# Reading the next expert's gates and indices three places later in a delta-rule and mixture-of-experts kernel

## The chip, the cores and the metric

The kernel runs on one core of a Trainium2 chip. The metric is the device time of one execution in microseconds (us). The engines are named as in the profile: PE (TensorE) multiplies matrices, with PEld for its weight loads, DVE (VectorE) and ACT (ScalarE) work on elements, POOL (GpSimd) here issues the scattered writes of the output, and SP (SyncE) issues the other DMAs, one after the other in the order of the program.

## The reference, cut to what matters

```python
def _attn_ref(q, k, v, beta):                    # B, H, S, D = 4, 8, 768, 48
    k_n = k / (norm(k) + 1e-06)
    for t in range(S):                           # a state of 48 x 48 per batch and head
        y[:, :, t] = q_t @ state
        state = state + beta_t * outer(k_t, v_t - k_t @ state)

def _moe_ref(x, w_gate, w1, w2):                 # x: 3072 tokens x 384, 8 experts
    expert_idx = argmax(x @ w_gate); gate_w = softmax(x @ w_gate)[chosen]
    for e in range(8):
        xe = x[expert_idx == e]
        out[mask] = gate_w * (maximum(xe @ w1[e], 0) @ w2[e])   # 384 -> 1024 -> 384
```

The outputs are 3072 rows of 384 floats. All arrays are float32.

## The kernel before, in words

The first 290 us or so compute the attention part, a block of 128 positions at a time, choose an expert for each token and scatter each token's row (384 features, 8 gate logits, 2 words of index) into DRAM, into a list per expert of 448 slots. Most rows lie in `xg`; those of the last blocks lie in `xt`. A part of expert 0 runs beside it. The change does not touch this stage.

The second stage runs the experts 0 to 7 one after the other. `ffn` of an expert is cut into places: the loop of line 1134 gives it twelve, `t` = 0 to 11. At places 0 to 7 PE makes one 128-row block of the hidden layer each (line 785, nine matmuls of 448 columns: float32 is done as three products of a high and a low part), ACT takes the ReLU of it as the high part (line 788) and DVE makes the low part (line 789). Five PSUM banks hold hidden blocks that wait for ACT and DVE. At places 8 to 10 PE makes the three output blocks (line 1092, 24 matmuls each; their last three take block 7 of the hidden layer), DVE transposes and scales them (lines 1094 and 1095), and POOL scatters them to the output. Experts 1 to 6 have 144 such matmuls each.

Two streams of preparation for the next expert are woven in by hand, and their order on each engine is that of the program:

- The weights. Each step of `pieces` takes one raw piece (512 KB of `w1` or 384 KB of `w2`, tile `w1r` or `w2r`), casts it on ACT (line 656, high part), subtracts on DVE (line 657, low part), and issues the load of the piece three ahead (line 672), which goes into the buffer just read. An expert has seven pieces, three of `w1` and then four of `w2`. The tuples `PC0`, `PC1`, `PC2` and `PC` say at which places a step comes, for experts 0, 1, 2 and the later ones. At places 0 to 7 it stands behind the place's ReLU, so a cast that waits for its piece holds up the next ReLU on ACT.
- The tokens. `tokens(e + 1)` steps at the places in `TOK`. In `load_blocks` the first step issues four reads of the main rows (`xr<-xg`, 168 KB each, line 711), at place 1. The second, at place 2, issues four reads of the last rows (`xs<-xt`, 24 KB each, line 730) and then the reads of gates and indices: eight (lines 732 to 734), alternately 17.5 KB from `xg` into `xr` and 2.5 KB from `xt` into `xs`, in runs of ten floats. For expert 7 they are three (lines 736 to 738). At place 8 DVE adds the last rows in (line 1041) and transposes, ACT and DVE split into high and low parts; at place 9 the gates and indices are used (lines 1066 and 771 to 776).

All of these DMAs go through SP. A weight load waits there for the subtraction that frees its buffer, and what stands behind it in the program waits with it.

Pieces are numbered through all experts from 0; expert 2's are 14 to 20 and expert 3's 21 to 27. Below, load 15 is the load of piece 15. At expert 1 the steps at places 0, 1, 2, 4, 6, 7, 8, 9, 10, 10 handle pieces 10 to 19 and issue loads 13 to 22. At expert 2 the steps at places 0, 1, 3, 4, 6, 8, 9, 10 handle pieces 20 to 27 and issue loads 23 to 30.

Of the kernel before, what the change touches and what calls it, by code (L numbers as in the profile page):

```python
# [40 lines left out]
def deltanet_moe(ctx, tc, q, k, v, beta, w_gate, w1, w2, out):  # L41
# [78 lines left out]
    DEF = 2  # L120
    FP = 10
    AH = 3
    TOK = (1, 2, 8, 8, 8, 8, 8, 8, 8, 9)
    PC = (1, 3, 4, 6, 8, 9, 10)
    EU = 18
    TS = 8
    TOK0 = (0, 8, 8, 8, 8, 9, 9, 9, 10)
    PC0 = (0, 1, 3)
    PC1 = (0, 1, 2, 4, 6, 7, 8, 9, 10, 10)
    PC2 = (0, 1, 3, 4, 6, 8, 9, 10)  # L130
# [500 lines left out]
    def run(gen, steps=1):  # L631

        for _ in range(steps):
            if next(gen, tiles) is tiles:
                return False
        return True
# [60 lines left out]
    def read(out, in_):  # L697
        ins = nc.sync.dma_start(out=out, in_=in_)
        for x in put:
            tc.add_manual_dep(ins.ins, x.name, mybir.DependencyInfo(mybir.DependencyClass.Sync, mybir.DependencyReason.DATA),  # L700
                              reason="rows of every scatter")
# [5 lines left out]
    def turned(dram, e, t0, t1, x):  # L707

        rows = dram[e * CAP + 32 * t0:e * CAP + 32 * t1, :]
        for a in range(4):  # L710
            read(x[32 * a:32 * a + 32], rows[:, 96 * a:96 * a + 96].rearrange("(n t) c -> t n c", t=32))

    def gates(dram, e, sm):
        tail = dram[e * CAP + NG * 128:e * CAP + NG * 128 + 64, DM:ROW]
        read(sm, tail.unsqueeze(0).broadcast_to([2, 64, ROW - DM]))

    def load_blocks(e):
        X = xq_[e % 2].tile([128, (NG + 1) * ROW if e % 2 == 0 else NX + NT_ * (E + 2)], F32, name=f"xr{e}", tag="xr")
        x = X[:, 0:NX].rearrange("p (n c) -> p n c", n=NT_)
        m = NT_ if e < E - 1 else NG + 1  # L720
        sm = X[:, NX:NX + m * (E + 2)].rearrange("p (g c) -> p g c", g=m)
        XR[e] = (x, sm)
        turned(xg, e, 0, NT_, x)
        yield
        n = NT_ - 4 * NG
        xs = xp_.tile([128, (96 + ROW - DM) * n], F32, name=f"xs{e}", tag="xs")
        y, ym = xs[:, 0:96 * n].rearrange("p (n c) -> p n c", n=n), xs[:, 96 * n:96 * n + ROW - DM]
        if e < E - 1:
            ym = xs[:, 96 * n:(96 + ROW - DM) * n].rearrange("p (n c) -> p n c", n=n)
        turned(xt, e, 4 * NG, NT_, y)  # L730
        if e < E - 1:
            for a in range(4):
                for z, dram, t0 in ((sm, xg, 0), (ym, xt, 4 * NG)):
                    read(z[32 * a:32 * a + 32], dram[e * CAP + 32 * t0:e * CAP + CAP, DM:ROW].rearrange("(n t) c -> t n c", t=32))
        else:
            gates(xg, e, sm[:, NG])
            gates(xt, e, ym)
            read(sm[:, 0:NG], xg[e * CAP:e * CAP + NG * 128, DM:ROW].rearrange("(g p) c -> p g c", p=128))
        yield
        add_last(e, (y, ym))  # L740
        XM[e] = sm[:, 4 * NG:] if e < E - 1 else sm[:, NG], ym
# [296 lines left out]
    def add_last(e, xs):  # L1038
        todo = ((XR[0][:, NG], xs),) if e == 0 else ((XR[e][0][:, 4 * NG:], xs[0]),)
        for x, y in todo:  # L1040
            nc.vector.tensor_tensor(out=x, in0=x, in1=y, op=ALU.add)

    def tokens(e, X):
        if e == 0:
            xs = load_last(e)
            X.extend(X0["x"])
            yield
            add_last(e, xs)
            X.append(smalls(e, G0, NG + 1, xp_))
            return  # L1050
        yield from load_blocks(e)
        xh = xp_.tile([128, KD, CAP], F32R, name=f"xh{e}", tag="xh", bufs=2)
        xl = xp_.tile([128, KD, CAP], F32R, name=f"xl{e}", tag="xl", bufs=2)
        X[0:0] = [xh, xl]
        yield
        x, xd = XR[e][0], []
        for i in range(2 * KD):
            d = (0, 1, 0, 2, 1, 2)[i]
            if i in (0, 1, 3):
                xd.append(xp_.tile([128, CAP], F32, name=f"xd{e}_{d}", tag="xd", bufs=2))  # L1060
                nc.vector.transpose(out=xd[d].rearrange("p (n t) -> p n t", n=NT_),
                                    in_=x.rearrange("p n (t k) -> p k n t", k=KD)[:, d])
            else:
                split(xh[:, d], xl[:, d], xd[d])
            yield
        nc.vector.tensor_tensor(out=XM[e][0], in0=XM[e][0], in1=XM[e][1], op=ALU.add)
        X.append(smalls(e, 0, NT_ if e < E - 1 else NG + 1, xp_))
# [63 lines left out]
    for e in range(E):  # L1131
        tok = tok1 if e == 0 else tokens(e + 1, XX[e + 1]) if e + 1 < E else iter(())
        main = ffn(e, WW[e], XX[e])
        for t in range(KF + NG + 1):
            if e == 0 and t == TS:
                run(tok0)
            run(tok, (TOK if e > 0 else TOK0).count(t))
            w = (PC0, PC1, PC2, PC)[min(e, 3)].count(t)
# [166 lines left out]
```

## Time and profile before

| | |
|---|---|
| median of 3 runs | 540.11 us (539.44 to 541.98) |
| the profiled execution, its own time | 533.12 us |
| its span, first to last instruction | 531.4 us |
| mean granted clock of PE | 0.981 |
| PE, DVE, ACT, POOL busy | 94%, 74%, 50%, 34% |
| DMA queue of SP: packets, MB | 168468, 67.06 |

The profile is of one execution. Its own time is 1.7 us over its span and 7.0 us under the median of the other runs. Busy shares are means over stages that differ; the expert stage is read below by itself.

### The profile page before, as it was taken

The numbers are of one execution on the slowest core, as the hardware profiler recorded it, in microseconds if no ns is written. First come the engines' busy times: TensorE is split into PE (matmuls) and PEld (weight loads), VectorE is DVE, ScalarE is ACT, GpSimd is POOL, SyncE is SP. The second block draws the span as 40 slices with busy tenths as digits, with TensorE's granted clock in tenths as the row PEclk, the third lists the DMA queues.
The fourth block names the chain that finished last, engine by engine and source line by source line (L and its number), as shares of the span: only waits on it lengthen the run. The fifth ranks groups of instructions, "written<-read, shape, count | busy, mean of one in ns | idle before, by whom it ended". The sixth has DMA issues, their size and how long they took to land.

```text
span 531.4 us, 17329 instructions
## 1 busy us (share of the span) xinstructions
PE 501.0 (94%) x7164; PEld 447.0 (84%) x7172; DVE 390.8 (74%) x1110; ACT 266.9 (50%) x496; POOL 181.7 (34%) x244
## 2 busy tenths in 40 slices
PE   7789899999999999788999999997999999999995
PEld 4657798899999887787899999985999999999995
DVE  5999969879999999446553484787777786878420
ACT  4636566667666554467532463554353536444120
POOL 8011221143233142323211110047271727365462
PEclk9999999999999999899999899997999999999998
DMA  6969789789576855645412557386765847483010
GB/s 133 151 149 227 171 210 217 151 199 175 127 184 134 183 131 119 209 101 201 143 65 90 107 145 157 115 209 162 178 170 143 180 115 165 142 189 114 19 44 29
DMA packets 173253, 77.76 MB, mean 146 GB/s; under 512 B 150786, under 2 KB 166864, under 8 KB 173172
## 3 DMA queue, kind: packets, MB, share of 16 engines
q1 hardware_dynamic: 168468, 67.06, 54.5%
q0 software_dynamic: 4704, 9.57, 5.3%
q8 instruction: 57, 0.93, 0.7%
q14 instruction: 24, 0.20, 0.1%
HBM read 53.02 MB, written 24.37 MB: 146 GB/s over the span
## 4 chain that ended last, share of the span: by engine, by line
PE 67%; DVE 20%; issue 4%; DMA 4%; ACT 3%; POOL 1%; SPq 0%; DVEq 0%; POOLq 0%; ACTq 0%
PE h L785 18%; PE y L1092 16%; PE y L795 4%; DVE lw L391 4%; PE yp L511 4%; PE pq L277 3%; PE yp L492 3%; PE ks L476 3%; PE xp L537 3%; PE ks L451 3%; PE pg L277 2%; DVE ta L380 2%; PE ks L462 2%; PE ku L501 2%; DVE tc L401 2%
## 5 line engine op out<-in xcount | busy, mean ns | idle before, releaser
L798 POOL DMA_INDIRECT out_dram<-yo,idx x90 | 97.9, 1087 | 134.9 <-DVE yo L1095 85.7
L1092 PE MATMUL y<-hx,w2h 128*128 128x448 f32 x288 | 85.7, 375 | 3.1 <-ACT hx L788 2.2
L302 POOL TENSOR_SCALAR_AFFINE_SELECT pm<-pm 128x512 f32<-128x512 f32 x48 | 31.2, 649 | 147.5 <-DVE lw L391 24.4
L788 ACT ACTIVATE hx<-h 128x448 fp32r<-128x448 f32 (+1 forms) x64 | 32.6, 519 | 61.7 <-PE h L785 58.3
L1092 PEld LDWEIGHTS y<-hx,w2h 128*128 128x128 f32 x288 | 55.3, 193 | 9.4 <-ACT hx L788 3.0
L785 PE MATMUL h<-xh,w1h 128*128 128x448 f32 x168 | 61.6, 366 | 1.0 <-DVE hx L789 1.0
L785 PE MATMUL h<-xl,w1h 128*128 128x448 f32 x168 | 61.5, 366 | 0.0
L785 PE MATMUL h<-xh,w1l 128*128 128x448 f32 x168 | 61.5, 366 | 0.0
L789 DVE SCALAR_TENSOR_TENSOR hx<-h,hx 128x448 fp32r<-128x448 f32 (+1 forms) x64 | 37.0, 587 | 32.1 <-ACT hx L788 32.1
L480 ACT COPY u<-ks 32x384 f32<-32x384 f32 x96 | 45.1, 470 | 23.5 <-PE ks L476 19.8
L1092 PE MATMUL y<-hx,w2l 128*128 128x448 f32 x144 | 53.5, 371 | 0.0
L657 DVE TENSOR_TENSOR w2l<-w2r,w2h 128x768 fp32r<-128x768 f32 x32 | 36.4, 1141 | 12.4 <-ACT w2h L656 12.0
L657 DVE TENSOR_TENSOR w1l<-w1r,w1h 128x1024 fp32r<-128x1024 f32 x24 | 29.4, 1226 | 14.1 <-ACT w1h L656 13.9
L656 ACT CAST w2h<-w2r 128x768 fp32r<-128x768 f32 x32 | 35.5, 1130 | 4.3 <-DMA w2r<-in_moe_w_dram 4.3
L785 PEld LDWEIGHTS h<-xh,w1h 128*128 128x128 f32 x168 | 31.5, 188 | 4.1 <-DVE hx L789 1.4
L391 DVE TENSOR_TENSOR lw<-lw,ta 128x31 f32<-128x31 f32 (+7 forms) x96 | 33.9, 353 | 0.3
L785 PEld LDWEIGHTS h<-xh,w1l 128*128 128x128 f32 x168 | 31.5, 188 | 2.8
L785 PEld LDWEIGHTS h<-xl,w1h 128*128 128x128 f32 x168 | 31.5, 188 | 2.7
L257 ACT COPY gg<-pg 128x512 f32<-128x512 f32 x48 | 25.8, 588 | 15.6 <-PE pg L277 15.4
L380 DVE TENSOR_TENSOR ta<-lg,lw 128x31 f32<-128x31 f32 (+7 forms) x96 | 33.4, 348 | 0.2
L277 PE MATMUL pq<-qt,kt 64*128 64x128 f32 x384 | 30.5, 292 | 2.1 <-ACT gg L257 1.2
L294 ACT COPY pm<-pq 128x512 f32<-128x512 f32 x48 | 25.8, 589 | 12.3 <-PE pq L277 12.3
(184 smaller groups left out, 1092.6 us busy)
## 6 DMA issues: line engine op xcount, KB each, us to landing
w1r<-in_moe_w_dram SPq DMA_DIRECT2D x24, 512.0 KB
w2r<-in_moe_w_dram SPq DMA_DIRECT2D x32, 384.0 KB
xg<-zrow SPq DMA_DIRECT2D x7, 788.0 KB
xr<-xg SPq DMA_DIRECT2D x28, 168.0 KB
kn<-in_k_dram SPq DMA_DIRECT2D x24, 192.0 KB
qn<-in_q_dram SPq DMA_DIRECT2D x24, 192.0 KB
xn<-row SPq DMA_DIRECT2D x10, 394.0 KB
ku<-in_k_dram SPq DMA_DIRECT2D x20, 192.0 KB
```

The costliest lines, as they stand in the source:

```text
L277: nc.tensor.matmul(pg[a][:, p], lhsT=kt[r, p], rhs=xt[r, p], start=True, stop=True, tile_position=(64 * a, 0), skip_group_check=True)
L302: ins = nc.gpsimd.affine_select(out=pm[:, hs], in_=pm[:, hs], compare_op=ALU.is_gt, fill=0.0, base=0, pattern=[[0, NP], [1, C]], channel_m ...
L380: nc.vector.tensor_tensor(out=x, in0=lg[:, rows, c:c + 1].broadcast_to([128, m, w]), in1=lw[:, c:c + 1, cols].broadcast_to([128, m, w]), o ...
L391: nc.vector.tensor_tensor(out=y, in0=y, in1=x, op=ALU.subtract)
L480: nc.scalar.copy(out=uview(n)[r], in_=ks[r])
L656: nc.scalar.copy(out=hi, in_=src)
L657: nc.vector.tensor_tensor(out=lo, in0=src, in1=hi.bitcast(F32), op=ALU.subtract)
L785: nc.tensor.matmul(ps, lhsT=w[:, d, fs], rhs=x_[:, d], start=(n == 0), stop=(n == len(terms) - 1))
L788: nc.scalar.activation(out=hh, in_=ps, func=AF.Relu)
L789: nc.vector.scalar_tensor_tensor(out=hl, in0=ps, scalar=0.0, in1=hh.bitcast(F32), op0=ALU.max, op1=ALU.subtract)
L798: ins = nc.gpsimd.indirect_dma_start(out=out.rearrange("n (a c) -> (n a) c", a=k), out_offset=bass.IndirectOffsetOnAxis(ap=idx, axis=0), i ...
L1092: nc.tensor.matmul(ps, lhsT=w[:, f, 128 * d:128 * d + 128], rhs=h[:, f], start=(n == 0), stop=(n == len(terms) - 1))
```

## The change

The generator `load_blocks` gets one more `yield`, between the reads of the last rows and the reads of gates and indices, and `TOK` one more place, 5. So the main rows are still read at place 1 and the last rows at place 2, and the gates and indices at place 5. `TOK0`, which does the same for expert 1 while expert 0 runs, gets a second 0, so that there both parts are issued at place 0 as before, in the same order.

```diff
-    TOK = (1, 2, 8, 8, 8, 8, 8, 8, 8, 9)
+    TOK = (1, 2, 5, 8, 8, 8, 8, 8, 8, 8, 9)
...
-    TOK0 = (0, 8, 8, 8, 8, 9, 9, 9, 10)
+    TOK0 = (0, 0, 8, 8, 8, 8, 9, 9, 9, 10)
...
         turned(xt, e, 4 * NG, NT_, y)
+        yield
         if e < E - 1:
             for a in range(4):
                 for z, dram, t0 in ((sm, xg, 0), (ym, xt, 4 * NG)):
```

## Rows read from the trace of the kernel before

**Rows 1.** The page's slices, 13.3 us each: PE's busy tenths, its granted clock.

```profile
PE   7789899999999999788999999997999999999995
...
PEclk9999999999999999899999899997999999999998
```

**Rows 2.** Windows from one expert's first matmul to the next's (experts 1, 2, 3).

```profile
core 0: us, PE busy (x) PEld busy (x) DVE busy (x) ACT busy (x) POOL busy (x), PEclk, DMA share, GB/s
311.39:340.48 29.09, 29.09 (x145) 26.86 (x145) 18.89 (x29) 14.41 (x20) 0.92 (x1) 1.00 0.59 151
340.48:378.44 37.96, 33.84 (x146) 28.95 (x145) 30.33 (x47) 18.29 (x24) 17.00 (x14) 0.91 0.62 161
378.44:407.68 29.24, 29.24 (x145) 27.02 (x145) 22.93 (x34) 13.70 (x19) 14.67 (x14) 1.00 0.63 164
```

**Rows 3.** Timeline of PE at expert 2: start, duration, in brackets the idle time before.

```profile
350.91 0.47 PE L785 MATMUL h<-xh,w1h 128*128 128x448 f32 x1 [0.98 <-DVE hx L789]
...
364.50 0.74 PE L1092 MATMUL y<-hx,w2h 128*128 128x448 f32 x1 [2.20 <-ACT hx L788]
...
365.82 1.12 PE L1092 MATMUL y<-hx,w2h 128*128 128x448 f32 x2 [0.21 <-DVE hx L789]
```

**Rows 4.** The chain that ended last, the one DMA on it at expert 2.

```profile
354.59 8.18 DMA w2r<-in_moe_w_dram
```

**Rows 5.** Timeline of ACT: casts of pieces 14, 15 and 24, ReLUs of block 7.

```profile
326.11 1.05 ACT L656 CAST w1h<-w1r 128x1024 fp32r<-128x1024 f32 x1 [1.29 <-DMA w1r<-in_moe_w_dram]
327.07 0.54 ACT L788 ACTIVATE hx<-h 128x448 fp32r<-128x448 f32 x1
332.47 1.05 ACT L656 CAST w1h<-w1r 128x1024 fp32r<-128x1024 f32 x1 [4.87 <-DMA w1r<-in_moe_w_dram]
...
362.80 1.21 ACT L656 CAST w2h<-w2r 128x768 fp32r<-128x768 f32 x1 [2.55 <-DMA w2r<-in_moe_w_dram]
363.92 0.53 ACT L788 ACTIVATE hx<-h 128x448 fp32r<-128x448 f32 x1
```

**Rows 6.** Timeline of SP's issues at expert 1, from place 2 on.

```profile
319.39 3.17 SPq L698 DMA_DIRECT2D xs<-xt  x4
322.60 0.42 SPq L698 DMA_DIRECT2D xr<-xg  x1
...
326.11 0.30 SPq L698 DMA_DIRECT2D xs<-xt  x1
...
327.92 0.48 SPq L698 DMA_DIRECT2D xs<-xt  x1
328.49 0.85 SPq L672 DMA_DIRECT2D w1r<-in_moe_w_dram  x2
```

**Rows 7.** Windows before and at load 15's landing, and at expert 2; columns as in 2.

```profile
326.11:328.49 2.38, 2.38 (x13) 2.21 (x12) 1.29 (x2) 1.50 (x2) 0.00 (x0) 1.00 0.19 11
328.49:332.47 3.98, 3.98 (x22) 3.69 (x21) 0.47 (x1) 0.00 (x0) 0.00 (x0) 1.00 0.74 222
...
351.99:362.80 10.81, 9.58 (x44) 7.74 (x43) 6.74 (x9) 4.74 (x8) 8.94 (x7) 1.00 0.92 198
```

**Rows 8.** Timeline of SP's issues at expert 2: load 24, the fourth gate read.

```profile
354.59 0.93 SPq L672 DMA_DIRECT2D w2r<-in_moe_w_dram  x1
...
362.79 0.30 SPq L698 DMA_DIRECT2D xs<-xt  x1
```

**Rows 9.** Timeline of DVE: expert 1's rows added; gates of experts 3 and 5 used.

```profile
307.37 0.36 DVE L1041 TENSOR_TENSOR xr<-xr,xs 128x192 f32<-128x192 f32 x1
...
373.33 0.17 DVE L1066 TENSOR_TENSOR xr<-xr,xs 128x20 f32<-128x20 f32 x1
...
431.26 0.17 DVE L1066 TENSOR_TENSOR xr<-xr,xs 128x20 f32<-128x20 f32 x1
```

**Rows 10.** Timelines of SP: last gate read for expert 1, and for expert 5.

```profile
307.52 0.47 SPq L698 DMA_DIRECT2D xs<-xt  x1
...
420.01 0.48 SPq L698 DMA_DIRECT2D xs<-xt  x1
```

## The prediction

> **What bounds the kernel now.** I began with the page's slices. In the expert stage, slices 24 to 39, PE is at 9 tenths in every slice but one: slice 28, from 359 to 372 us, stands at 7 and its granted clock at 7 [rows 1]. (Slice 40 is the tail behind the last expert.) So a change in this stage is worth only what it does to that slice, or what new hole it makes elsewhere. Windows from one expert's first matmul to the next's give the size: experts 1 and 3 take 29.09 and 29.24 us with PE busy throughout, expert 2 takes 37.96, at a mean clock of 0.91 [rows 2]. Expert 2 loses 37.96 - 29.17 = 8.8 us.
>
> PE's timeline says what it waits for there: 0.98 us for DVE, which has not yet freed the first of five hidden blocks, at 350.91; 2.20 us for ACT's ReLU at 364.50; DVE's low part of the same block at 365.82 [rows 3]. The chain that ended last goes at this place through one DMA, a weight load from 354.59 to its landing [rows 4]. ACT shows the same from its side: the cast of piece 24 waited 2.55 us for that load, began at 362.80, and the ReLU of block 7 had to stand behind it until 363.92 [rows 5]. So preparation of expert 3 arrives late and holds up expert 2's own ReLU.
>
> Why is it late? I followed ACT back. At expert 1 it waited 4.87 us for load 15, until 332.47 [rows 5]. From there the steps stand in one row: each load waits for the subtraction three pieces before, each subtraction for its cast. And load 15 left SP only at 328.49, behind the eight reads of gates, which SP took from 322.60 to 328.40 to issue [rows 6]. In the last 2.4 us of this the DMA engines moved 11 GB/s, with loads 15 to 17 in the air they moved 222 [rows 7]. The bandwidth was there; the loads were not issued.
>
> SP's pauses between these reads follow a pattern: the fourth read goes out at 326.11, when load 14 lands and its cast begins [rows 5, 6], and at expert 2 the fourth goes out at 362.79, when load 24 lands [rows 5, 8]. Both times it is the eighth DMA behind that load. I read this as: a DMA of SP is not issued before the one eight places ahead has landed.
>
> **The change, part by part.** Nothing is removed or added in work. At each of experts 1 to 5, eight reads move from place 2 to place 5, at expert 6 three: 43 DMAs. In SP's order each group moves behind two weight loads (places 2 and 4 at expert 1, places 3 and 4 later). POOL's queue is not touched. At expert 0 both steps fall on place 0, in the old order: zero.
>
> *Expert 1.* Load 15 takes the first gate read's turn: 322.60 instead of 328.49 [rows 6]. From issue to landing it took 332.47 - 328.49 = 4.0 us [rows 5, 6], which from 322.60 gives 326.6. But load 14 lands ahead of it at 326.11, and 512 KB behind that at 222 GB/s [rows 7] take at most 2.3 us: 328.4. The cast of piece 15 stands behind block 7's ReLU, which ends at 327.07 + 0.54 = 327.6 [rows 5]. So the cast begins between 327.6 and 328.4 and not at 332.47: the preparation runs 4.1 to 4.9 us earlier. I take 4.4, nearer the late end, because load 16 shares the engines.
>
> The gate reads are then issued behind load 16. By the pattern of eight, the seventh waits for load 15 and the eighth for load 16, so load 17 leaves at about 330.5 instead of 329.4. With the same 4.0 us it lands at 334.5. Its cast comes only at place 9, which PE itself begins at 311.39 + 96 x 0.203 = 330.9 [rows 2], and on ACT and DVE behind all of place 8: the transposes and splits of expert 2's tokens and piece 16. That work hides it; without it, what it is late would be taken off the 4.4 us.
>
> *Expert 2.* With the whole row of steps 4.4 us earlier, PE's wait at 350.91 (0.98) is gone. What is late next is load 24. It stands behind the four main reads and load 23 in both orders, so it only moves with its row: from 362.80 to 358.4. How late is that for PE? At 29.17/144 = 0.203 us per matmul, the last of the first output block (72 + 23 matmuls behind 340.48 [rows 2]) is due at 340.48 + 95 x 0.203 = 359.8. It ran at 365.82 [rows 3], 6.0 late. So 6.0 of the 8.8 us are waiting and the other 2.8 are the clock; that a mean of 0.91 over 37.96 us is 3.4 us of missing clock [rows 2] bounds this. Afterwards the wait is 6.0 - 4.4 = 1.6 us, in two pieces for high and low part, each below the 0.98 that left the clock at 1.00 in the window that followed [rows 3, 7]. So I count no fall of the clock, and the gain is 8.8 - 1.6 = 7.2 us.
>
> Two unknowns stand around load 24. Three gate reads were in the air behind it and no longer are, which can only help: at most the 1.6 us that remain. Against it, load 25, and later load 26, now come right behind it. Do later DMAs take a share from earlier ones? While load 15's 512 KB landed, the queue moved 3.98 x 222 = 884 KB [rows 7], so 372 KB of the loads behind went with it: yes. The bounds are nothing and both loads' 768 KB at the 198 GB/s of this stretch [rows 7], 3.9 us. I take nothing, as load 25 leaves only after the last rows' reads, when load 24 is mostly through.
>
> The Trainium skill (DMA: Bandwidth & Descriptors, "Queues, rings and completion order") says that each DMA engine takes descriptors in the order of the ring, while a later one may finish its write first. By that alone the loads behind would cost load 24 nothing and the sum would stay 7.2; the 372 KB show that landings do mix, so the bound stays.
>
> *Experts 3 to 6.* The later loads leave about 4 us sooner, the reads later. PE is full there, so no gain. The cover is the time between the reads and their use: expert 5's last gate read is issued at 420.01 and its gates are used at 431.26, 11.3 us later [rows 9, 10]. Two hidden blocks, the distance from place 3 to place 5, are 2 x 9 x 0.203 = 3.7 us; so some 7.6 us remain: no cost. The adding of last rows at place 8 does not wait for the gates, though they share its tiles: for expert 1 it ran at 307.37, before the last gate read was even issued at 307.52 [rows 9, 10].
>
> **Sum.** 533.12 - 7.2 = 525.9 us for the profiled execution. The other runs' median is 7.0 us above it, for which the trace gives no reason; I take the same microseconds off: 540.1 - 7.2 = 532.9. The likeliest case's own range, with shifts of 3.5 to 5.5, is 532 to 534.5.
>
> **The rivals.**
> *The hole closes wholly.* Load 24 lands 1.6 us sooner than I say, for instance because no gate reads are in the air with it. For it: the reserve of DMA bandwidth at expert 1. Against: the main reads still lie before it. 540.1 - 8.8 = 531.3. Chance 0.25.
> *The hole shrinks, but the clock falls all the same.* If loads 25 and 26 cost load 24 about 0.6 us, PE's wait is 2.2, as long as the one after which the clock halved [rows 3]. Then 2.8 + 0.6 come back: 7.2 - 3.4 = 3.8, 536.3 us. Chance 0.14.
> *No difference.* Loads 25 and 26 take their full share: 1.6 + 3.9 = 5.5 us of waiting and 2.8 of clock against 8.8 leave 0.5 us; the stretch before load 24's landing ran at 0.92 of the DMA engines [rows 7], which speaks for it. Against: load 25 is issued behind load 24. 539.6 us. Chance 0.13.
> *Slower.* The gates come late. Their use at place 9 blocks DVE, and with it output blocks and the next ReLUs. This decides from about 7.6 us of landing time after the last issue; PE feels it only when its five free hidden banks, 5 x 1.83 us, are used up, less some 3 us until DVE's first low part, so from 13 or 14 us. Each further microsecond costs five at experts 2 to 6; 2 us beyond would give 540.1 - 7.2 + 10 = 543. Against: expert 3's gates, the latest now with their fourth read out at 362.79, were used at 373.33 with no wait [rows 8, 9]. Chance 0.06.
> The Trainium skill (DMA: Bandwidth & Descriptors, "Rules for kernel authors") would issue a DMA early and wait for it late, which speaks for this rival; here the trace shows early reads holding back loads that are more urgent.
>
> **How the numbers follow.** 0.42 is left for my forecast. A measurement of this kernel tells about 0.5% (2.7 us) from no change. Faster by more: 0.25 + 0.42 + 0.14 = 0.81; within it 0.13; slower 0.06. The range runs from the wholly closed hole with the runs' own lower spread (531.3 - 0.7 = 530.6) to the fallen clock with most of their upper spread (536.3 + 1.5 = 537.8); what is left out is about 2 in 10.
>
> **What would show it.** Right: ACT's wait of 4.87 us before piece 15 shrinks below 1 us; load 15 leaves SP before 324; between the last rows' and the gates' issues stand two weight loads; expert 2's block takes 30 to 31.5 us; clock 1.00 in slice 28. Wrong: cast 15 moves but load 24 still lands near 362 (DMA bandwidth, not order, was the limit); or a new wait at lines 1066 or 771 for a DMA; or expert 1, whole until now, gets a hole because load 14 shares with loads 15 and 16 and lands over 2.7 us later (block 7's ReLU, over at 327.6, is due at 311.39 + 93 x 0.203 = 330.3).

## The result, and the profile after

| | before | changed |
|---|---|---|
| median of 4 runs each, us | 539.78 (535.40 to 541.98) | 531.50 (528.53 to 533.22) |
| ratio, 95% interval | | 0.987 (0.9825 to 0.9915) |
| the profiled execution, its own time | 533.12 | 531.65 |

A ratio compares the fast executions of the two kernels only, leaving out the slow ones, which lie over 1.5% above the fastest, so 0.987 is not the quotient of the two medians. By the ratio the change is worth 539.8 x 0.013 = 7.0 us (4.6 to 9.4 by its interval); 7.2 were forecast, and the median of 531.5 stands 1.4 us under the 532.9. The two profiled executions, though, differ by only 1.5 us. Both facts have to come out of the trace.

The page's slices of the changed kernel, PE and its granted clock, to be held against [rows 1]:

```profile
PE   7799899999999999898999899999999999999975
...
PEclk9899999999999999999999999999999999999979
```

Slice 28 is full now, at full clock, and stays so to slice 38. A new dent stands in slice 39, near the end. Windows by expert, as in [rows 2], give the size of both: experts 1, 2 and 3, and from expert 7's first matmul to the end of the span.

```profile
core 0: us, PE busy (x) PEld busy (x) DVE busy (x) ACT busy (x) POOL busy (x), PEclk, DMA share, GB/s
311.19:340.43 29.24, 29.24 (x145) 27.02 (x145) 22.43 (x38) 17.03 (x24) 0.92 (x1) 1.00 0.64 164
340.43:370.03 29.60, 29.60 (x146) 26.96 (x145) 24.94 (x36) 15.84 (x21) 15.01 (x14) 1.00 0.69 185
370.03:399.28 29.25, 29.25 (x146) 27.03 (x145) 22.95 (x35) 13.65 (x19) 15.58 (x14) 1.00 0.66 162
...
487.17:529.90 42.73, 33.30 (x161) 30.65 (x159) 8.46 (x16) 6.68 (x12) 18.38 (x24) 0.91 0.09 28
```

Expert 2's block fell from 37.96 [rows 2] to 29.60: 8.4 us, and PE is busy for all of the 29.60. The last stretch took 42.73 us; in the profile of before the same stretch takes 35.82:

```profile
495.58:531.40 35.82, 29.95 (x160) 28.46 (x159) 8.46 (x16) 6.69 (x12) 18.52 (x24) 0.95 0.10 34
```

So 6.9 us went again, and 8.4 - 6.9 = 1.5 is what the pair of profiles shows. What the 6.9 are, runs 1 and 9 below tell: they come with the execution, not with the change.

ACT's timeline, to be held against [rows 5]: the casts of pieces 14, 15 and 24, the ReLU behind the last, and two ReLUs of expert 7.

```profile
326.16 1.05 ACT L656 CAST w1h<-w1r 128x1024 fp32r<-128x1024 f32 x1 [1.55 <-DMA w1r<-in_moe_w_dram]
327.12 0.54 ACT L789 ACTIVATE hx<-h 128x448 fp32r<-128x448 f32 x1
327.85 1.06 ACT L656 CAST w1h<-w1r 128x1024 fp32r<-128x1024 f32 x1 [0.19 <-DMA w1r<-in_moe_w_dram]
...
356.14 1.23 ACT L656 CAST w2h<-w2r 128x768 fp32r<-128x768 f32 x1 [2.11 <-DMA w2r<-in_moe_w_dram]
357.27 0.55 ACT L789 ACTIVATE hx<-h 128x448 fp32r<-128x448 f32 x1
...
505.36 0.54 ACT L789 ACTIVATE hx<-h 128x448 fp32r<-128x448 f32 x1 [4.38 <-remote]
508.95 0.54 ACT L789 ACTIVATE hx<-h 128x448 fp32r<-128x448 f32 x1 [3.04 <-remote]
```

The wait before piece 15 went from 4.87 to 0.19 us. Piece 24's cast still waits, 2.11 us, but 15.7 us after the block's start and no longer 22.3, in time for PE: no wait of PE is left in the blocks of experts 2 to 6. SP's issues at expert 1, as in [rows 6], and last one of expert 2:

```profile
322.64 1.57 SPq L672 DMA_DIRECT2D w1r<-in_moe_w_dram  x2
324.81 0.33 SPq L698 DMA_DIRECT2D xr<-xg  x1
326.16 0.33 SPq L698 DMA_DIRECT2D xs<-xt  x1
...
328.51 0.42 SPq L698 DMA_DIRECT2D xr<-xg  x1
329.44 0.30 SPq L698 DMA_DIRECT2D xs<-xt  x1
...
356.14 0.33 SPq L698 DMA_DIRECT2D xs<-xt  x1
```

Loads 15 and 16 stand ahead of the gate reads. The pattern of eight shows again: the second read goes out at 326.16 with the cast of piece 14, and at expert 2 the second at 356.14 with that of piece 24; before, it was the fourth each time [rows 6, 8], because loads 15 and 16, or 25 and 26, now stand between.

### The profile page after: what moved, and what is told of

Same layout as the page of the kernel before. It is cut to its first block, busy times and chain, and to the rows that moved or that the text cites. A ratio compares the mean times of both kernels' runs of the same rounds, so it can differ in the third digit from the quotient of the medians.

```text
span 529.9 us, 17343 instructions
## 1 busy us (share of the span) xinstructions
PE 500.8 (95%) x7172; PEld 446.0 (84%) x7172; DVE 388.2 (73%) x1110; ACT 267.0 (50%) x496; POOL 181.2 (34%) x244
## 4 chain that ended last, share of the span: by engine, by line
PE 71%; DVE 15%; ACT 4%; DMA 3%; issue 3%; POOL 2%; another core or an unknown queue 1%; SPq 0%; POOLq 0%; ACTq 0%; DVEq 0%
PE h L786 21%; PE y L1093 17%; PE y L796 4%; PE pg L277 4%; PE yp L492 3%; PE yp L511 3%; PE ks L476 3%; PE pq L277 3%; PE xp L537 3%; PE ks L451 3%; PE ks L462 2%; DVE lw L391 2%; DMA kn<-in_k_dram 2%; PE pt L230 2%; PE wm L650 1%
## 5 line engine op out<-in xcount | busy, mean ns | idle before, releaser
L1093 PE MATMUL y<-hx,w2h 128*128 128x448 f32 x288 | 82.8, 365 | 0.0
L1093 PEld LDWEIGHTS y<-hx,w2h 128*128 128x128 f32 x288 | 54.0, 188 | 4.4
L786 PEld LDWEIGHTS h<-xh,w1h 128*128 128x128 f32 x168 | 31.5, 188 | 2.8
L786 PEld LDWEIGHTS h<-xh,w1l 128*128 128x128 f32 x168 | 31.5, 188 | 2.8
L786 PEld LDWEIGHTS h<-xl,w1h 128*128 128x128 f32 x168 | 31.5, 188 | 2.8
L277 PE MATMUL pg<-kt 64*128 64x128 f32 x384 | 29.6, 292 | 2.6 <-ACT gg L257 2.2
L277 PE MATMUL pq<-qt,kt 64*128 64x128 f32 x384 | 29.6, 285 | 2.0 <-ACT gg L257 1.2
```

Source lines behind the costliest of these rows:

```text
L277: nc.tensor.matmul(pg[a][:, p], lhsT=kt[r, p], rhs=xt[r, p], start=True, stop=True, tile_position=(64 * a, 0), skip_group_check=True)
L786: nc.tensor.matmul(ps, lhsT=w[:, d, fs], rhs=x_[:, d], start=(n == 0), stop=(n == len(terms) - 1))
L1093: nc.tensor.matmul(ps, lhsT=w[:, f, 128 * d:128 * d + 128], rhs=h[:, f], start=(n == 0), stop=(n == len(terms) - 1))
```

## The experiments

The times of one kernel spread by up to 4% on the chips used here, so a ratio's interval is wide and the block of expert 2 in the profile is the sharper measure. The table gives it for all runs but run 10, with the time in it that PE was idle (the window's length less PE's busy time), and the cast of piece 15 after expert 1's first matmul and of piece 24 after expert 2's first matmul (ACT's timeline, minus the block's start), which is where loads 15 and 24 landed if ACT waited for them. A block's bounds are read to within one matmul, 0.2 us. Each row gives one profiled execution, and the ratio of the timed runs; runs 1 to 4, 5 to 8, and 9 and 10 stood on one chip each. Edits are shown against the changed kernel.

| run | gate reads | piece 15, us | piece 24, us | expert 2's block, us | PE idle in it, us | ratio to before (95%) |
|---|---|---|---|---|---|---|
| first profile of before | place 2 | 21.1 | 22.3 | 37.96 | 4.1 | 1 |
| 1, before again | place 2 | 21.0 | 21.8 | 36.12 | 4.1 | 1.0025 (0.9961 to 1.0089) |
| 3 | 2 at expert 1, then 5 | 21.2 | 21.1 | 35.98 | 4.2 | 0.9979 (0.9925 to 1.0032) |
| 4 | 2, in sixteen halves | 26.8 | 26.3 | 41.55 | 5.8 | 1.0135 (1.0091 to 1.0180) |
| changed | 5 | 16.7 | 15.7 | 29.60 | 0 | 0.9870 (0.9825 to 0.9915) |
| 5, changed again | 5 | 16.4 | 16.4 | 29.72 | 0 | 0.9940 (0.9880 to 0.9999) |
| 9, changed again | 5 | 16.7 | 16.8 | 30.10 | 0.2 | none |
| 2 | 5 at expert 1, then 2 | 16.4 | 17.3 | 30.66 | 0.6 | 0.9896 (0.9792 to 0.9999) |
| 6 | 3 | 16.7 | 17.7 | 31.08 | 0.9 | 0.9900 (0.9853 to 0.9947) |
| 7 | 8 | 16.5 | 16.8 | 30.10 | 0.6 | 0.9943 (0.9903 to 0.9983) |
| 8 | 5, in sixteen halves | 16.6 | 15.8 | 29.60 | 0 | 0.9956 (0.9914 to 0.9997) |

**Run 1: the kernel before again.** No edit.

> The kernel before, unchanged, to see a second profile of it and what two runs of one kernel differ by. Both theories: ratio 1.00 within 0.4%. Expert 2's block again takes 37 to 39 us, with load 24 landing about 22 us after the block's start (362.8 - 340.5 in the first profile) and piece 15's cast waiting about 4.9 us at expert 1. Open: whether ACT's pauses of 4.4 and 3.0 us at expert 7, which the profile of the changed kernel has and that of before has not, come with the execution and not with the change; then they may appear here too, and would explain the 7 us between the profiled execution of before and its other runs.

The windows of expert 2 and of the last stretch, and ACT at expert 7:

```profile
338.60:374.72 36.12, 32.05 (x146) 27.53 (x145) 28.91 (x46) 18.28 (x24) 15.33 (x14) 0.95 0.59 163
493.83:535.60 41.77, 32.16 (x161) 29.51 (x159) 8.46 (x16) 6.68 (x12) 18.38 (x24) 0.93 0.09 29
```

```profile
514.31 0.54 ACT L788 ACTIVATE hx<-h 128x448 fp32r<-128x448 f32 x1 [6.55 <-remote]
515.79 0.54 ACT L788 ACTIVATE hx<-h 128x448 fp32r<-128x448 f32 x1 [0.94 <-remote]
```

Two things follow. The hole at expert 2 varies between executions of one kernel: 36.1 here, under the 37 to 39 that were expected, and 38.0 in the first profile. PE was idle for the same time in both, 36.12 - 32.05 = 4.07 us here and 4.12 [rows 2]; what differs is how long it was busy, at a mean granted clock of 0.95 against 0.91. So the blocks of before and of the changed kernel lie 6.0 to 8.4 us apart, by the pair that one takes. And ACT's pauses at expert 7 stand in the kernel before too: the last stretch takes 41.77 us instead of 35.82. The first profile of before, at 533.12, lacked them. The 7.0 us between it and its other runs, for which the prediction found no reason, are about this size; that they are the cause is likely and not shown, as the other runs left no trace.

**Run 2: only expert 1's reads moved.**

```diff
-            run(tok, (TOK if e > 0 else TOK0).count(t))
+            run(tok, (TOK0 if e == 0 else TOK if e == 1 else (1, 2, 2, 8, 8, 8, 8, 8, 8, 8, 9)).count(t))
```

> Only the reads for expert 2 (issued at expert 1) stand at place 5; all later ones stay at place 2. My theory, that the gain is load 15 leaving before the gate reads at expert 1: all of the gain, ratio to before 0.984 to 0.990, expert 2's block 29.5 to 31 us, cast of piece 15 waiting under 1 us. Rival, that the reads moved at expert 2, away from loads 24 to 26, give the gain: expert 2's block stays above 35 us and the ratio above 0.994.

**Run 3: all but expert 1's moved.** The same line with `TOK if e > 1`.

> The other half: the reads stand at place 5 at experts 2 to 6, and at place 2 at expert 1. My theory: piece 15 waits 4.9 us as before, load 24 lands within 1.5 us of 22 us after expert 2's start, expert 2's block takes 36.5 to 39 us and the ratio is 0.996 to 1.003. Rival, that the gate reads behind load 24 delay its landing: it lands 1.5 us or more sooner, the block takes 33 to 36 us and the ratio is 0.990 to 0.996.

Expert 2's window, first of run 2, then of run 3:

```profile
341.43:372.09 30.66, 30.03 (x145) 26.80 (x145) 24.09 (x36) 15.54 (x21) 15.57 (x14) 1.00 0.69 179
```

```profile
340.20:376.18 35.98, 31.74 (x146) 28.08 (x145) 29.43 (x47) 18.29 (x24) 15.89 (x14) 0.95 0.62 166
```

With the changed kernel and before, these are all four combinations. Load 24, after the block's start: 22.0 us with nothing moved (mean of two), 17.3 with expert 1's reads moved, 21.1 with the later ones, 16.3 with both (mean of three). Expert 1's move gives 4.7, the later one 0.9, both 5.7: they add up. But load 24 scatters by 0.5 us between the two executions with nothing moved and by 1.1 us between the three of the changed kernel, so the 0.9 is not clear of the scatter. In the block, run 2 has nearly all of the gain, and run 3 is no better than run 1: 35.98 us is under the 36.5 to 39 that I expected and just inside the rival's 33 to 36, but run 1, with nothing moved, has 36.12, and PE is idle for 4.24 us as in before. So the rival that the move at expert 2 gives the gain falls; at most about a microsecond is left for it. Run 3's profile also has pauses of ACT at expert 5, 7.9 us together, behind the block read here; they make that execution a long one, 545.74 us.

**Run 4: twice as many reads at place 2, same bytes.**

```diff
-    TOK = (1, 2, 5, 8, 8, 8, 8, 8, 8, 8, 9)
+    TOK = (1, 2, 2, 8, 8, 8, 8, 8, 8, 8, 9)
...
-                    read(z[32 * a:32 * a + 32], dram[e * CAP + 32 * t0:e * CAP + CAP, DM:ROW].rearrange("(n t) c -> t n c", t=32))
+                    m = (NT_ - t0) // 2
+                    for i in range(2):
+                        read(z[32 * a:32 * a + 32, i * m:i * m + m],
+                             dram[e * CAP + 32 * (t0 + i * m):e * CAP + 32 * (t0 + i * m + m), DM:ROW].rearrange("(n t) c -> t n c", t=32))
```

> Each of the eight gate reads is cut in two halves, all sixteen at place 2: the same bytes in the same runs of ten floats, but twice as many issues on SP. My theory, that SP's issue time of some 0.47 us per read is what holds load 15: it leaves SP 8 x 0.47 = 3.8 us later than in before, piece 15's wait grows from 4.9 to 8 to 9 us, expert 2's block grows by 3 to 6 us to 41 to 44, ratio 1.005 to 1.012. Rival, that the many small packets are the cost and not the issues: the same packets, so the block stays at 37 to 39 us and the ratio within 0.3% of 1.

SP's issue of loads 15 and 16, the cast of piece 15, and the windows of experts 1 and 2:

```profile
334.71 0.84 SPq L672 DMA_DIRECT2D w1r<-in_moe_w_dram  x2
```

```profile
338.47 1.05 ACT L656 CAST w1h<-w1r 128x1024 fp32r<-128x1024 f32 x1 [8.40 <-DMA w1r<-in_moe_w_dram]
```

```profile
311.72:342.50 30.78, 29.68 (x145) 26.76 (x144) 15.22 (x25) 12.00 (x17) 0.92 (x1) 1.00 0.58 155
342.50:384.05 41.55, 35.75 (x145) 29.64 (x146) 30.44 (x48) 19.34 (x27) 14.40 (x14) 0.88 0.56 148
```

The same bytes in the same runs, issued in twice as many DMAs, make the hole 3.6 to 5.4 us larger and the kernel 1.35% slower, a little over the 0.5 to 1.2% that I expected. Piece 15 waits 8.4 us, as expected. Load 15 left 334.71 - 311.72 = 23.0 us after expert 1's start, though, 5.9 later than the 17.1 of before, where 3.8 were expected: 3.6 came with the sixteen reads, which took 9.4 us (325.23 to 334.61) where eight took 5.8, and the other 2.3 were there before the first of them. The reads issued at expert 0 were doubled as well, and loads 10 to 13 and the main reads behind them left later too, which also made expert 1 some 1.5 us longer. So the number of issues is the cost, and this run counts it at two places.

**Runs 5 to 8.** Run 5 is the changed kernel; the others change the place, and run 8 the reads as in run 4.

```diff
-    TOK = (1, 2, 5, 8, 8, 8, 8, 8, 8, 8, 9)
+    TOK = (1, 2, 3, 8, 8, 8, 8, 8, 8, 8, 9)      (run 6)
+    TOK = (1, 2, 8, 8, 8, 8, 8, 8, 8, 8, 9)      (run 7)
```

> The changed kernel, unchanged, beside the next three and for a second profile. Both theories: ratio to before 0.983 to 0.991, expert 2's block 29.3 to 30.5 us, piece 15's wait under 1 us. ACT's pauses without a releaser in the profile, seen by now in the kernel before too, may stand at any expert or nowhere.

> The gate reads at place 3: at expert 1 they stand behind load 15 (place 2) but still ahead of load 16 (place 4). My theory, that load 15's place alone decides, since piece 16 is cast only behind place 8's token work: all of the gain, expert 2's block 29.3 to 31 us, ratio as the changed kernel's within 0.4%; load 16 leaves SP near 329 and lands near 333, just before its cast at about 334. Rival, that both loads have to be ahead: piece 16's cast waits 2 us or more for its load, expert 2's block takes 32 to 35 us, and the ratio lies in the middle between the changed kernel's and 1.

> The gate reads as late as place 8, one place before they are used. My theory: what counts is that they follow the loads; some 2 us remain between their last issue and their use in full blocks, DVE may wait up to 2 us for them, and PE does not feel it behind its five hidden banks: expert 2's block 29.2 to 30.2 us, all later blocks below 29.7, ratio as the changed kernel's within 0.4%. Rival, the slower one of the prediction, that late gates block DVE: waits of 3 us or more at the lines that use them, blocks of 30.5 us and more at experts 2 to 6, and a ratio at least 0.6% above the changed kernel's.

> Each gate read in two halves as in the fourth run, sixteen issues, but at place 5 as in the changed kernel. My theory, that SP's issue time costs only what more urgent loads it holds: expert 2's block 29.3 to 31 us, ratio as the changed kernel's within 0.4%, where the same sixteen at place 2 cost 1.35% of before. Rival, that sixteen issues cost SP and the DMA engines their time wherever they stand: expert 2's block grows by 3 us or more, to 32.5 or above, and the ratio rises by 0.5% or more over the changed kernel's.

Run 5's ratio, 0.994, lies outside the 0.983 to 0.991 that I expected; its block is as expected, with PE busy throughout:

```profile
343.63:373.35 29.72, 29.72 (x146) 26.89 (x145) 24.23 (x35) 15.57 (x21) 15.83 (x14) 1.00 0.71 184
```

Run 6: load 16 leaves SP 17.9 us after expert 1's start and its cast waits for no load, as SP and ACT show:

```profile
331.80 0.38 SPq L672 DMA_DIRECT2D w1r<-in_moe_w_dram  x1
```

```profile
336.55 1.05 ACT L656 CAST w1h<-w1r 128x1024 fp32r<-128x1024 f32 x1
```

One place later, behind load 15 alone, gives nearly all of the gain; the block is 31.08, just above my bound of 31, and load 24 comes at 17.7, near run 2's 17.3. This run also tests the pattern of eight. One load stands between the last rows' and the gates' reads instead of none or two, so by the pattern the third gate read has to wait for load 14, where it was the fourth before and the second in the changed kernel. It does: the third read goes out as piece 14's cast begins.

```profile
328.88 0.30 SPq L698 DMA_DIRECT2D xr<-xg  x1
```

```profile
328.89 1.05 ACT L656 CAST w1h<-w1r 128x1024 fp32r<-128x1024 f32 x1 [1.59 <-DMA w1r<-in_moe_w_dram]
```

Run 7, at expert 2: the last read is issued at 362.38 and the gates are used at 366.49 with no wait before it:

```profile
362.38 0.48 SPq L698 DMA_DIRECT2D xs<-xt  x1
```

```profile
366.49 0.17 DVE L1067 TENSOR_TENSOR xr<-xr,xs 128x20 f32<-128x20 f32 x1
```

So even a distance of 4.1 us is enough, the blocks of experts 3 to 6 take 29.1 to 29.6 us, and the slower rival does not begin at place 8. Run 8: sixteen reads at place 5 leave the block at 29.60, where the same sixteen at place 2 made it 41.55. So the issue time on SP costs here only what waits behind it. Among runs 5 to 8 the ratios lie between 0.990 and 0.996 with intervals of 0.4 to 0.6% either way; they rank nothing.

**Runs 9 and 10: ACT's pauses.** Run 9 is the changed kernel; run 10 lets DVE make expert 7's ReLU.

```diff
-        nc.scalar.activation(out=hh, in_=ps, func=AF.Relu)
+        if dve:                                    # e == E - 1
+            nc.vector.tensor_scalar(out=hh, in0=ps, scalar1=0.0, scalar2=None, op0=ALU.max)
+        else:
+            nc.scalar.activation(out=hh, in_=ps, func=AF.Relu)
```

> The changed kernel once more, beside the next one and with more rounds: ratio to before 0.985 to 0.993, expert 2's block 29.3 to 30.5 us; ACT's pauses at the last hidden blocks of expert 7, in the five profiles of this order of reads so far 5.4 to 8 us together, are there again.

> The changed kernel, and at expert 7 DVE makes the ReLU's high part too (a maximum with 0, into the same tile), where it has little else to do. The pauses of ACT at expert 7 have no releaser in the profile and come in nearly all executions. Theory one, that they are ACT's own: expert 7's hidden blocks follow PE at once, the stretch from its first matmul to the span's end is about 36 us as in the first profile of before, instead of 42 to 43, and the kernel is 0.6 to 1.3% faster than the changed one. Theory two, that something shared stops whichever engine stands there: DVE pauses or PE waits 3 us or more at the same place, and the time equals the changed kernel's within 0.4%. Nothing is left out of the computation.

Run 9's expert 2, then the windows from expert 7's first matmul to the end, run 9 and run 10:

```profile
337.40:367.50 30.10, 29.88 (x146) 26.90 (x145) 24.41 (x36) 15.81 (x21) 14.72 (x14) 1.00 0.72 182
```

```profile
484.60:520.50 35.90, 30.00 (x161) 28.51 (x159) 8.46 (x16) 6.69 (x12) 18.54 (x24) 0.96 0.10 34
```

```profile
490.20:526.10 35.90, 29.98 (x161) 28.51 (x159) 13.45 (x24) 2.32 (x4) 18.59 (x24) 0.97 0.10 34
```

Inconclusive: this time, against what I expected, the changed kernel's profiled execution had no pause either, so the two stretches are equal. The times say a little more. Run 9's six runs fall into two groups, 519.5 and 522.2, and four from 529.3 to 530.4, a gap of about the pauses' size, so no ratio is given for them; run 10's are 522.0 to 527.8, median 526.4. Run 10's ratio is 0.9897 (0.9841 to 0.9954). It is a version faster than before, but not shown to be faster than the changed kernel.

## Why the prediction was right, point by point

**What bounds it.** Right: the hole at expert 2 was what the change could touch. Experts 1 and 3 kept their 29.1 to 29.3 us.

**Expert 1.** Right, with its sizes. Load 15 left SP at 322.64 (forecast 322.60) and landed at 327.85 (327.6 to 328.4). Measured from expert 1's start the shift is 21.1 - 16.7 = 4.4 us, as forecast. Load 17 left at about 329.8 (forecast 330.5) and was in time. That load 15's place behind the reads is the cause is shown from both sides: run 2 has the gain with nothing else moved, run 4 makes the loss larger by holding load 15 longer.

**The pattern of eight.** It predicted the new order: the second read waits for load 14, and the eighth (329.44) follows load 16. With no, one and two loads between, it was the fourth, the third (run 6) and the second read that waited for load 14, always the eighth DMA behind it. Whether the chip or the program's own waits make the pattern, no run shows.

**Expert 2.** The mechanism was right, one term was too large: the 1.6 us of waiting that I left to PE. It is 6.0 - 4.4, and the 6.0, the lateness of one matmul, is not all waiting. PE's idle time in the block was 37.96 - 33.84 = 4.1 us [rows 2]; for the rest of the lateness it counts as busy, and 33.84 - 29.17 = 4.7 of the 8.8 us are longer busy time, not 2.8. Run 2, which has expert 1's shift alone, leaves PE 0.63 us idle and not 1.6. The changed kernel leaves it 0, 0 and 0.2 us: what its block takes over the 29.2 of its neighbours is, but for these 0.2, PE being busy at a granted clock of 1.00. So the block undercut the 30 to 31.5 us that I had named as the sign in two of three profiles. Load 24 also came sooner than I put it, at 358.4 or 17.9 us after the block's start: 15.7 to 16.8, and 17.3 in run 2. What I called an unknown and took as nothing, the gate reads that are no longer behind load 24, can be worth the other 0.9 us (runs 2, 3 and the two kernels), though it is not clear of the scatter; whatever loads 25 and 26, which took their place, cost is inside this difference. The stretch from load 23's issue to load 24's landing moved 198 GB/s before [rows 7], and now 244:

```profile
347.40:356.14 8.74, 8.74 (x44) 7.92 (x43) 6.77 (x9) 4.84 (x8) 6.91 (x7) 1.00 1.01 244
```

So what happened at expert 2 is nearer to the rival of the wholly closed hole than to my forecast. The clock did not fall, as counted.

**Experts 3 to 6.** Right: 29.25, 29.05, 29.24 and 29.60 us.

**The rivals.** The hole closes wholly: nearly so, as said. No difference: the loads behind load 24 did not hold it back, it came sooner than forecast. The clock: 1.00. Slower by late gates: not even at place 8 (run 7).

**The sum.** 7.2 us were forecast; the block gave 8.4 in the first pair of profiles and 6.5 against run 1, the timed runs 7.0 in the first comparison, and in run 5 on another chip 0.6%, about 3 us, with an interval that ends at 6.4; the two intervals overlap. That 7.0 came so near to 7.2 is in part luck: against the profile that I forecast from, the gain was larger than forecast because no wait was left, and in run 1 the hole itself was smaller, at a higher clock. Taking the same microseconds off the other runs, for which I had no reason, is not contradicted: ACT's pauses stand in most profiled executions of both kernels, and at expert 7 they take 7.5 us in run 1 and 7.4 in the changed kernel.

## What to carry to other kernels

An engine that issues its DMAs in program order is a place where small, patient transfers can hold up large, urgent ones: look at what stands ahead of each late load in that engine's timeline, and whether the DMA engines are idle meanwhile (11 GB/s here, in the 2.4 us before load 15 was issued). The harm showed some 20 to 30 us later, one expert on, so a chain of waits has to be followed back past the first DMA that it names. Where one profile and the other runs differ by more than their spread, profile the old kernel twice before explaining the difference.

## What the runs showed of the hardware that I had not expected

ACT pauses at the last hidden blocks of expert 7, with PE's results ready and no releaser in the profile ("remote"). The pauses sum up to 7.4 or 7.5 us in runs 2, 5, 6, 7 and 8 and in the first profile of the changed kernel, and 9 to 15 us with others at expert 3, 5 or 6 in runs 1, 3 and 4; they were absent in the first profile of before, in run 9 and in run 10. They may make up much of the spread of this kernel's times; only profiled executions show them, so this is not shown. Their cause stays open.

The time that the gate reads took on SP was one of issue, not of data: eight of them hold 80 KB and took 5.8 us, and sixteen with the same 80 KB took 9.4 us in run 4.
